# Erf's batches one step sooner than the mean's logarithms, and the forms of x one step behind their norm

## The chip, the cores and the metric

The kernel runs on one core of one Trainium2 chip. The metric is device time in microseconds of one execution. Small differences are told as a ratio with a 95% interval. Such a ratio is not quite the ratio of the medians quoted beside it.

## The reference, cut to what matters

```python
kv  = np.einsum('bhsd,bhse->bhde', k, v)          # 8 batches, 8 heads, 576 rows, 64 wide
out = np.einsum('bhsd,bhde->bhse', q, kv)
rms = np.sqrt(np.mean(out * out, axis=-1, keepdims=True) + 1e-06)
x   = (out / rms * g_norm)                        # -> 4608 x 512
h   = x @ w_in                                    # -> 4608 x 2048
sp  = np.maximum(h, 0.0) + np.log1p(np.exp(-np.abs(h)))   # softplus
y   = (h * erf(sp)) @ w_out                       # -> 4608 x 512
```

## The kernel before

The 4608 rows are worked on in nine groups of 512. The first two groups (T = 0 and 1) multiply in full precision; in their time the weights are unpacked (first group) and cut into three forms for the later groups (second group). A group has 16 steps, so there are 32 steps n; step n computes block n of h, and the projection of block n-5. Between them stand the pieces of the next group's attention: a pair of heads takes four steps, and its norm stands at the head of the step after them.

ScalarE's functions come from three tables here: softplus, erf, and one that has both exp and ln. Each change of table is an instruction. So erf is applied in batches of four blocks, and the mean's Ln and Exp stand between two loads.

```python
def mean():                                  # cut; step 4p+3
    nc.tensor.matmul(ms, lhsT=mean_w, rhs=st.pop("hi"), start=True, stop=False)
    nc.tensor.matmul(ms, lhsT=mean_w, rhs=st.pop("lo"), start=False, stop=True)
    exp_ln_table()
    nc.scalar.activation(r, ms, AF.Ln, bias=eps_col)
    nc.scalar.activation(r, r, AF.Exp, scale=-0.5)
    nc.scalar.activation(u, r, AF.Square)
    softplus_table()

def norm():                                  # step 4p+4: three VectorE operations
    ...                                      # L341 reads ms, L344, L353 reads o and writes x

def split():                                 # the three forms of x: one on ScalarE (L378),
    if T >= FIRST:                           # two on VectorE (L381, L382)
        thirds(st.pop("x"), *(x_forms[T][:, i, p, :] for i in range(3)))
```

```python
for n in range(FIRST * FC + 1):              # cut; FC = 16, BATCH = 4, LAG = 5
    for piece in steps[f][0]:
        piece()                              # attention of the next group, kv and qt first
    ...                                      # weights of the next steps
    nc.vector.tensor_tensor(out=hs[done], in0=hs[done], in1=ss[done], op=ALU.mult)  # done = n-4
    h_ps = ...                               # 4 matmuls (8 passes)
    nc.scalar.copy(h, h_ps)
    nc.scalar.activation(s, h, AF.Softplus)
    ...                                      # second group: forms of weights, two ahead of erf, one behind
    if f % BATCH == BATCH - 1:
        for i in range(n - BATCH + 1, n + 1):
            nc.scalar.activation(ss[i], ss[i], AF.Erf)
        softplus_table()
    ...
    project(f2, hs[n - LAG], last)
```

Two PSUM banks serve kv (the products of k and v), qt (q, transposed), se (kv applied to q) and ms (the mean's product) in turn: kv of a new pair takes the bank of the old ms, qt that of the old se.

## Time and profile before

| | |
|---|---|
| time | 991.83 us, median of 3 (991.8 to 993.1); in later rounds 989.9 to 990.1 |
| TensorE busy | 951.9 us of 991.4 (96%) |
| ScalarE, VectorE busy | 618.7 us (62%), 736.6 us (74%) |
| the 32 steps of the change | from 31.2 us, h of step 0, to 280.0 us, the first product of the part after it |
| TensorE's bracketed waits in steps 4 to 28 | 8.16 us: 1.49 + 0.59 + 3.45 in steps 4 and 5, 0.37 + 0.34 + 1.92 in step 24 and at the head of 25 |

A bracketed wait is the idle time that a profile line gives in brackets before an instruction, with what ended it. The page is read in this way: TensorE's busy share says that the end moves only with TensorE's gaps and its clock; the gaps in order of time say where; the engine named behind a gap says which stream to read next. The lines themselves are in the prediction.

### The profile page before, as it was taken

To read this page: it belongs to the slowest core of one execution; us is meant where nothing else is said; L and a number is where in the kernel's file an instruction comes from. 1 tells how busy PE (TensorE), PEld (TensorE's weight loads), DVE (VectorE), ACT (ScalarE), POOL (GpSimd) and SP (SyncE) were. 2 spreads that over 40 slices of the span, in tenths; PEclk is the share of its full clock that TensorE was granted. 3 is DMA by queue.
4 is the path that set the end of the run, shared out by engine and by line. 5 is a ranking of instruction groups with operands and counts; after the bars stand their busy time and mean duration, and the time that the engine had idled before them with its cause. 6 is when DMAs were issued, how large, how long until landed. Compare 5 with 4: busy or idle time off the path is not lost.

```text
span 991.4 us, 11745 instructions
## 1 busy us (share of the span) xinstructions
PE 951.9 (96%) x4328; PEld 681.5 (69%) x4328; DVE 736.6 (74%) x1047; ACT 618.7 (62%) x822; POOL 2.4 (0%) x10
## 2 busy tenths in 40 slices
PE   6779999989999999999999999999999999989997
PEld 4334444444477878787878787878787787768885
DVE  2887896657368887777777777888777787776666
ACT  3688776676466666666666666666666666665551
POOL 0000000000000000000000000000000000000000
PEclk9899999999999999999999999999999999999998
DMA  9755516679369976998689878977787678657952
GB/s 278 229 165 165 164 40 246 273 300 376 135 225 362 374 267 233 292 374 294 244 256 371 307 269 248 368 298 280 246 331 250 248 264 343 236 204 284 363 203 74
DMA packets 100936, 259.76 MB, mean 262 GB/s; under 512 B 44048, under 2 KB 57360, under 8 KB 100880
## 3 DMA queue, kind: packets, MB, share of 16 engines
q1 hardware_dynamic: 99248, 256.73, 72.4%
q10 hardware_dynamic: 1568, 2.29, 0.8%
q8 instruction: 34, 0.56, 0.2%
q14 instruction: 22, 0.18, 0.1%
q0 software_dynamic: 64, 0.00, 0.0%
HBM read 224.40 MB, written 34.60 MB: 261 GB/s over the span
## 4 chain that ended last, share of the span: by engine, by line
PE 72%; DVE 15%; ACT 7%; DMA 3%; issue 2%; SPq 0%; DVEq 0%; ACTq 0%
PE n_ps L427 34%; PE m_ps L427 17%; PE h_ps L582 7%; PE o_ps L464 6%; DVE h L718 3%; PE se_ps L304 3%; DVE e L412 2%; PE qt_ps L298 2%; PE kv_ps L276 1%; DMA w_out_parts<-w_out 1%; DVE u L344 1%; DVE x L353 1%; DVE u L341 1%; DVE e L407 1%; ACT L105 1%
## 5 line engine op out<-in xcount | busy, mean ns | idle before, releaser
L427 PE MATMUL n_ps<-x_forms,w_in_parts 128*128 128x512 f32 x896 | 234.2, 403 | 3.0 <-ACT x_forms L378 2.8
L427 PE MATMUL n_ps<-w_out_parts,g_forms 128*128 128x512 f32 x928 | 232.7, 393 | 3.0 <-DMA w_out_parts<-w_out 3.0
L427 PEld LDWEIGHTS n_ps<-w_out_parts,g_forms 128*128 128x128 f32 x928 | 175.6, 189 | 41.1 <-DMA w_out_parts<-w_out 3.8
L427 PEld LDWEIGHTS n_ps<-x_forms,w_in_parts 128*128 128x128 f32 x896 | 167.3, 189 | 47.6 <-issue 9.1
L702 ACT ACTIVATE s<-h 128x512 f32<-128x512 f32 x112 | 71.0, 634 | 200.1 <-DVE h L412 200.1
L427 PE MATMUL m_ps<-w_out_parts,g_forms 128*128 128x512 f32 x464 | 125.0, 391 | 0.0
L582 PE MATMUL h_ps<-xT,w_in_sb 128*128 128x512 f32 x256 | 121.2, 617 | 4.0 <-DVE qT L341 2.7
L427 PE MATMUL m_ps<-x_forms,w_in_parts 128*128 128x512 f32 x448 | 120.8, 392 | 0.0
L412 DVE TENSOR_TENSOR h<-m_ps,h 128x512 f32<-128x512 f32 x112 | 77.1, 688 | 50.4 <-ACT h L700 47.1
L381 DVE TENSOR_TENSOR g_forms<-h,g_forms 128x1024 fp32r<-128x1024 f32 x58 | 70.9, 1223 | 46.9 <-ACT g_forms L378 46.6
L464 PE MATMUL o_ps<-w_out_sb,h_sb 128*128 128x512 f32 x224 | 100.5, 592 | 0.0
L427 PEld LDWEIGHTS m_ps<-w_out_parts,g_forms 128*128 128x128 f32 x464 | 87.8, 189 | 18.4
L427 PEld LDWEIGHTS m_ps<-x_forms,w_in_parts 128*128 128x128 f32 x448 | 84.6, 189 | 17.7
L582 PEld LDWEIGHTS h_ps<-xT,w_in_sb 128*128 128x128 f32 x256 | 49.8, 198 | 63.4 <-issue 55.2
L412 DVE TENSOR_TENSOR e<-m_ps,e 128x512 f32<-128x512 f32 x116 | 80.3, 692 | 17.5 <-PE m_ps L427 9.3
L407 DVE SCALAR_TENSOR_TENSOR e<-n_ps,e 128x512 f32<-128x512 f32 x88 | 60.3, 686 | 28.8 <-PE n_ps L427 28.8
L464 PEld LDWEIGHTS o_ps<-w_out_sb,h_sb 128*128 128x128 f32 x224 | 42.5, 190 | 53.2 <-issue 49.5
L700 ACT ACTIVATE h<-n_ps 128x512 f32<-128x512 f32 x112 | 65.6, 586 | 17.3 <-PE n_ps L427 17.2
L382 DVE SCALAR_TENSOR_TENSOR g_forms<-g_forms 128x1024 fp32r<-128x1024 f32 x58 | 71.1, 1225 | 2.0
L378 ACT ACTIVATE g_forms<-h 128x1024 fp32r<-128x1024 f32 x58 | 61.2, 1054 | 10.0 <-DVE h L718 8.5
L718 DVE TENSOR_TENSOR h<-h,s 128x1024 f32<-128x1024 f32 x56 | 65.9, 1219 | 0.0
L105 ACT ACT_TABLE_LOAD x45 | 57.7, 1283 | 0.8
(82 smaller groups left out, 950.8 us busy)
## 6 DMA issues: line engine op xcount, KB each, us to landing
w_out_parts<-w_out SPq DMA_DIRECT2D x116, 768.0 KB, 7.5
w_in_parts<-w_in SPq DMA_DIRECT2D x112, 768.0 KB, 6.5
w_in<-w_new SPq DMA_DIRECT2D x16, 768.0 KB, 4.3
w_out<-w_new SPq DMA_DIRECT2D x16, 768.0 KB, 5.2
k_sb<-in_k_dram SPq DMA_DIRECT2D x29, 288.0 KB, 4.9
v_sb<-in_v_dram SPq DMA_DIRECT2D x29, 288.0 KB, 5.7
q_sb<-in_q_dram SPq DMA_DIRECT2D x32, 256.0 KB, 5.1
w_raw<-in_moe_w_out_dram SPq DMA_DIRECT2D x8, 1024.0 KB, 4.9
```

The costliest lines, as they stand in the source:

```text
L105: nc.scalar.preload_act_table_set("softplus")
L378: nc.scalar.activation(high, x, AF.Copy, scale=1.0 + 2.0**-13)
L381: nc.vector.tensor_tensor(out=low, in0=x, in1=high.bitcast(FP32), op=ALU.subtract)
L382: nc.vector.scalar_tensor_tensor(out=both, in0=low.bitcast(FP32), scalar=SHIFT, in1=high.bitcast(FP32), op0=ALU.mult, op1=ALU.add,)
L407: nc.vector.scalar_tensor_tensor(out=out_, in0=ps, scalar=scale, in1=out_, op0=ALU.mult, op1=ALU.add)
L412: nc.vector.tensor_tensor(out=out_, in0=ps, in1=out_, op=ALU.add)
L427: nc.tensor.matmul(ps, lhsT=weights(form, k), rhs=moving(form, k), start=(form == forms[0] and k == 0), stop=(form == forms[-1] and k == 3),)
L464: nc.tensor.matmul(o_ps[j], lhsT=g[:, j * P : j * P + P], rhs=w_out_sb[:, f, :], start=(f == 0), stop=last,)
L582: nc.tensor.matmul(h_ps, lhsT=w_in_sb[:, c, f * P : f * P + P], rhs=xT[T][:, c, :], start=(c == 0), stop=(c == KC - 1),)
L700: nc.scalar.activation(h[:, i], n_ps, AF.Copy, scale=SHIFT - 1.0)
L702: nc.scalar.activation(s[:, i], h[:, i], AF.Softplus)
L718: nc.vector.tensor_tensor(out=h[:, part], in0=h[:, part], in1=s[:, part], op=ALU.mult)
```

## The change

The intent: erf's batch stood in the same step as the mean, between the mean's table loads and the copy of qT that TensorE needs next. One step sooner, it should be out of the way of that copy. And the forms of x, which made VectorE wait for ScalarE in the step of the norm, are to come a step later.

```diff
-                steps[BATCH * p + BATCH][0][:0] = [norm, split]
+                steps[BATCH * p + BATCH][0][:0] = [norm]
+                if p < NP - 1:
+                    steps[BATCH * p + BATCH + 1][0].insert(0, split)
@@
+    erf_steps = (*range(2, FIRST * FC - BATCH, BATCH), FIRST * FC - BATCH, FIRST * FC - 1)
+    to_erf = []
@@
-            if f % BATCH == BATCH - 1:
-                for i in range(n - BATCH + 1, n + 1):
-                    nc.scalar.activation(ss[i], ss[i], AF.Erf)
+            to_erf.append(s)
+            if n in erf_steps:
+                for s in to_erf:
+                    nc.scalar.activation(s, s, AF.Erf)
+                to_erf.clear()
                 softplus_table()
```

The batches are then in steps 2, 6, ... 26, 28 and 31 in place of 3, 7, ... 31.

## The prediction

> **What bounds the kernel now.** I read the page's totals, then the slices, then TensorE's gaps in order of time through the part that the change touches, then ScalarE's and VectorE's order around each gap. In the totals (busy us, share of the span, instructions) TensorE is busy almost throughout:
>
> ```profile
> PE 951.9 (96%) x4328; PEld 681.5 (69%) x4328; DVE 736.6 (74%) x1047; ACT 618.7 (62%) x822; POOL 2.4 (0%) x10
> ```
>
> So only what opens or closes a gap of TensorE, or lowers its clock, moves the end. The change touches the first two groups: 32 steps, from about 31 to 278 us. A step is one block of h (8 MATMULs, 3.43 us), one block of the projection (another 3.43 us) and a piece of the next group's attention. A pair of heads takes four steps: its products (kv, qt) in step 4p, its application (se) in 4p+1, its halves in 4p+2, its mean in 4p+3, and its norm at the head of 4p+4. I number steps by counting ScalarE's copies of h (step 3 at 56.49 us, step 14 at 140.25, step 24 at 218.91). TensorE in order of time (start, duration, work, and in brackets the gap before it and what ended it) shows the only real gaps of group one after step 3:
>
> ```profile
> 53.95 0.92 PE L276 MATMUL kv_ps<-v_sb,k_sb 96*64 96x64 f32 x24 [1.49 <-DVE u L341]
> 55.47 0.66 PE L298 MATMUL qt_ps<-ident,q_sb 128*128 128x128 f32 x4 [0.59 <-DVE xT L353]
> ...
> 63.17 1.12 PE L304 MATMUL se_ps<-qT,bd_kv 128*128 128x512 f32 x2 [3.45 <-ACT qT L299]
> 64.13 5.29 PE L582 MATMUL h_ps<-xT,w_in_sb 128*128 128x512 f32 x8
> ```
>
> and of group two:
>
> ```profile
> 209.75 0.92 PE L276 MATMUL kv_ps<-v_sb,k_sb 96*64 96x64 f32 x24 [0.37 <-DVE u L341]
> ...
> 211.27 0.66 PE L298 MATMUL qt_ps<-ident,q_sb 128*128 128x128 f32 x4 [0.34 <-DVE x L353]
> ...
> 220.71 0.43 PE L303 MATMUL kv_ps<-qT_last,bd_kv 128*128 128x64 f32 x2 [1.92 <-DVE qT_last L294]
> ...
> 222.24 4.95 PE L582 MATMUL h_ps<-xT,w_in_sb 128*128 128x512 f32 x8
> ```
>
> Two things are to be seen. First, kv waits for the norm's first operation (L341) and qt for its last (L353), since they take the PSUM banks that these read; se waits for the copy of qT (L299), which in step 4 stands behind the erf batch. Second, after the gaps of 3.45 and 1.92 us eight MATMULs take 5.29 and 4.95 us in place of 3.60. So each of those gaps costs a further 1.7 to 1.8 us of clock. The 1.49 us gap cost none (the next eight: 3.60).
>
> ScalarE in order of time around the end of group one shows what is to be swapped:
>
> ```profile
> 140.85 0.63 ACT L594 ACTIVATE s_sb<-h_sb 128x512 f32<-128x512 f32 x1
> 141.50 1.28 ACT L102 ACT_TABLE_LOAD   x1
> 142.80 0.69 ACT L333 ACTIVATE rms_r<-ms_ps,eps_col 128x512 f32<-128x512 f32 x1
> ...
> 144.18 0.63 ACT L335 ACTIVATE u<-rms_r 128x512 f32<-128x512 f32 x1
> 144.83 1.28 ACT L105 ACT_TABLE_LOAD   x1
> 146.12 0.59 ACT L593 COPY h_sb<-h_ps 128x512 f32<-128x512 f32 x1
> ...
> 147.39 1.28 ACT L607 ACT_TABLE_LOAD   x1
> 148.68 2.19 ACT L607 ACTIVATE s_sb<-s_sb 128x512 f32<-128x512 f32 x4
> 150.89 1.28 ACT L105 ACT_TABLE_LOAD   x1
> 152.18 0.59 ACT L299 COPY qT<-qt_ps 128x512 f32<-128x512 f32 x1
> ```
>
> An erf batch with its two table loads is 1.28 + 2.19 + 1.28 = 4.75 us. It stands now after the mean and before the copy of qT.
>
> VectorE in order of time shows the cost of the early forms of x, which sit in its stream waiting for ScalarE, which is in its erf batch:
>
> ```profile
> 183.92 0.69 DVE L381 TENSOR_TENSOR x_forms<-x,x_forms 128x512 fp32r<-128x512 f32 x1 [7.36 <-ACT x_forms L378]
> ...
> 218.57 0.69 DVE L381 TENSOR_TENSOR x_forms<-x,x_forms 128x512 fp32r<-128x512 f32 x1 [7.36 <-ACT x_forms L378]
> ```
>
> The second of them is the cause of the 1.92 us gap: the copies of kv and of the q tail stand behind it.
>
> **What the Trainium skill says.** "ScalarE: Activation LUTs", section "What ACT_TABLE_LOAD costs", has about 1283 ns for a load and 1380 ns of drain besides. The trace has 45 loads of 1283 ns, but no drain: the softplus before 141.50 ends at 141.48, and the Ln starts at 142.80. I take 1.28. "TensorE: Matmul & The Clock Gate", section "Architectural detail: the array is 16× 32×32, not 1× 128×128", says that ScalarE and VectorE run their queues strictly in order. The trace agrees (the 7.36 us above), and so order is what this change is about. Its section "Part 1: The HAM clock gate (the "warmup" mystery)" says that TensorE falls to half clock after an idle window of about 3.4 us and that the window runs freely. The size fits here (1.7 us lost), while a gap of 1.92 us was enough, so I treat gaps between 1.5 and 3 us as a matter of chance.
>
> **The change part by part.** No arithmetic is removed. The erf batches (before: 8, in steps 3, 7, ... 31) become 9, in steps 2, 6, ... 26, 28 and 31: two more loads, 2.6 us of ScalarE late in group two, where it has idle stretches of 2.8 to 5.6 us, so nothing on the path. What moves: in each pair of steps 4.75 us pass from behind the mean (ahead of the qT copy) to ahead of it. The qT copy comes no later; Ln, Exp, Square, the norm, and with it kv and qt, come 4.75 us later, less what ScalarE idled there waiting for the mean's product. I replay each boundary with the durations of the rows.
>
> Step 4: three erfs, so 1.28 + 1.65 + 1.28 = 4.2 us. The Square ends at 57.4 in place of 53.2, kv starts at 58.2, qt at 59.7, h at 60.2. The gap becomes one of 5.7 us and the clock falls there. The softplus of step 3 ends at 62.0 and the qT copy at 62.5, while TensorE is in its slow h (60.2 to about 65.3). So the 3.45 us wait is gone, taken by the longer one: the projection starts at about 69.5 against 69.26. +0.2 us.
>
> Step 8: ScalarE had idled 1.36 us there, so the norm comes 3.4 us later; its first operation ends at 86.4 (kv is due at 87.0), its last at 87.9 (qt due at 88.0). Nothing. Step 12 likewise, 3.4 us later, qt at 118.54 against 118.40: +0.1.
>
> Step 16: no idling, so the Square ends at 144.81 + 4.75 = 149.56. VectorE, which was the later one at 147.0, now waits. Its first operation ends at 150.3, kv starts then in place of 148.01 (gap 2.3 us), the last ends at 151.8, qt starts at 151.86 in place of 149.25. +2.6 us, and I give a fall of the clock 6 chances in 10: +1.0.
>
> Step 20: Square at 179.2 in place of 174.3, since one form of a weight also lies behind the batch; kv at 179.95 in place of 178.86, qt at 181.46 in place of 179.71. +1.75 us.
>
> Step 24: here the split's move earns. VectorE no longer stands 7.36 us in step 20, so the weights' forms go out about 3.5 us sooner, and ScalarE's waits for them in steps 21 and 22 (3.80, 1.28, 1.27 us for transfers) mostly go, which pays for most of the erf batch. In TensorE's own time I get kv 0.95 us late and qt 0.35, a loss of 1.3 us. Before: 0.37 + 0.34 + 1.92 and about 1.8 of clock, 4.45. So −3.15 us.
>
> Step 28: Square ends at 244.5 in place of 240.0; kv at 245.25 in place of 244.75, qt at 246.75 in place of 245.60. +1.15 us.
>
> Sum: 0.2 + 0.1 + 2.6 + 1.0 + 1.75 − 3.15 + 1.15 = 3.65 us. After 280 us nothing moves but the start.
>
> **The rivals.** One: the shorter wait of the copy of qT is all gain, and the norm has room enough; then steps 4 and 24 give back 3.45 + 1.7 and 4.45, and the time is about 982 to 985. For it speaks that steps 8, 12, 20 and 28 have 3.5 to 4.0 us between the norm and kv. Against it: the batch is 4.75 us, and step 16 has 2.5 us. Two: the wait only changes its place, as I reckon for step 4, and in all the clock falls twice more than I count (steps 16 and 20): about 998 to 1000. That the gaps now are single waits between long stretches of work speaks for it. Three: steps 21 to 23 are bound by transfers (they move 400 to 440 GB/s around 190 to 205 us), so that the earlier forms do not come sooner; then step 24 keeps a gap of 3.4 us for kv and its fall of the clock, and the time is about 999. Against it: VectorE held them back for 7.36 us first.
>
> **Range and chances.** 991.83 + 3.65 = 995.5 us. Each fall of the clock is worth 1.7 us, three are in doubt (steps 16, 20, 24), and step 24 itself by 3 us either way: 990.0 to 1000.0 eight times in ten. A change of 2% would be 19.8 us, more than all gaps touched together (about 10 us before): within 2% 0.98, faster 0.01, slower 0.01.
>
> **What would show it.** 47 table loads in place of 45. TensorE's wait for the qT copy in step 5 gone, and one of about 5.7 us for L341 at kv in step 4. New waits for L341 and L353 at steps 16, 20 and 28 of about 2.3 + 0.3, 1.1 + 0.7 and 0.5 + 0.6 us. No wait for L294 in step 24, and no 4.95 us row after it. VectorE's two waits of 7.36 us for x_forms down to under 2. I would be wrong if kv starts in step 16 without a gap, or if step 24 still has one of over 2 us.

## The result, and the profile after

The changed kernel took 999.3 us (median of 4, 996.19 to 1000.61) against 991.82 us: ratio 1.0072, 95% interval 1.0044 to 1.0101, that is about 7.1 us more.

TensorE of the changed kernel in order of time, columns as in the prediction, first group (step 4, the se of step 5, step 16):

```profile
57.48 1.55 PE L276 MATMUL kv_ps<-v_sb,k_sb 96*64 96x64 f32 x24 [5.76 <-DVE u L341]
...
59.90 5.24 PE L587 MATMUL h_ps<-xT,w_in_sb 128*128 128x512 f32 x8
...
65.15 1.08 PE L304 MATMUL se_ps<-qT,bd_kv 128*128 128x512 f32 x2
...
150.83 0.92 PE L276 MATMUL kv_ps<-v_sb,k_sb 96*64 96x64 f32 x24 [2.32 <-DVE u L341]
...
152.35 1.12 PE L298 MATMUL qt_ps<-ident,q_sb 128*128 128x128 f32 x4 [0.34 <-DVE xT L353]
153.26 4.65 PE L587 MATMUL h_ps<-xT,w_in_sb 128*128 128x512 f32 x8
```

and second group (steps 20, 24 and 28):

```profile
184.60 0.92 PE L276 MATMUL kv_ps<-v_sb,k_sb 96*64 96x64 f32 x24 [1.11 <-DVE u L341]
...
187.02 4.84 PE L587 MATMUL h_ps<-xT,w_in_sb 128*128 128x512 f32 x8
...
218.55 0.92 PE L276 MATMUL kv_ps<-v_sb,k_sb 96*64 96x64 f32 x24 [1.11 <-DVE u L341]
...
220.86 4.98 PE L587 MATMUL h_ps<-xT,w_in_sb 128*128 128x512 f32 x8
...
251.88 0.92 PE L276 MATMUL kv_ps<-v_sb,k_sb 96*64 96x64 f32 x24 [0.46 <-DVE u L341]
```

The 3.45 us wait of se is gone and a 5.76 us wait of kv has come. Where before only one pair boundary of the second group waited, all now do, and for the norm (L341). Behind the waits of steps 4, 16, 20 and 24 the next block of h takes 4.65 to 5.24 us in place of 3.60. ScalarE of the changed kernel around step 15 shows why the norm is late: erf's batch and both of its loads are now ahead of the Ln.

```profile
143.25 2.19 ACT L613 ACTIVATE s_sb<-s_sb 128x512 f32<-128x512 f32 x4
145.46 1.28 ACT L105 ACT_TABLE_LOAD   x1
146.75 1.28 ACT L102 ACT_TABLE_LOAD   x1
148.04 0.69 ACT L333 ACTIVATE rms_r<-ms_ps,eps_col 128x512 f32<-128x512 f32 x1
...
149.43 0.63 ACT L335 ACTIVATE u<-rms_r 128x512 f32<-128x512 f32 x1
```

The two traces can be set side by side from the first block of h (31.19 us before, 30.44 after), by the start of the work that follows each boundary (the last column is what the waits leave over, about the excess of the slow rows):

| boundary | predicted | measured | of it waits | of it clock (about) |
|---|---|---|---|---|
| step 4 and 5 | +0.2 | +0.98 | +0.2 | +0.8 |
| step 8 and 12 | +0.1 | +0.20 | +0.2 | 0 |
| step 16 | +3.6 | +4.13 | +2.66 | +1.5 |
| step 20 | +1.75 | +3.49 | +1.7 | +1.8 |
| step 24 | −3.15 | −1.46 | −1.18 | −0.3 |
| step 28 | +1.15 | +1.20 | +1.05 | 0 |
| sum | +3.65 | +8.54 | | |

The bracketed waits of these steps are 12.62 us after and 8.16 before: 4.46 more. My own terms without those for the clock come to 0.2 + 0.1 + 2.6 + 1.75 + (1.3 − 2.63) + 1.15 = 4.47. So the replay of the waits was right in these two profiles, and what was missed is clock. The span rose by 5.8 us, not 8.54: the changed kernel's first step began 0.75 us sooner, and the part after the 32 steps took 709.4 us against 711.4, a difference that a later run puts down to chance (the second profile of the kernel before, below).

### The profile page after: what moved, and what is told of

The parts are those of the page before. It is cut to its first block, busy times and chain, and to the rows that moved or that the text cites. A ratio compares the mean times of both kernels' runs of the same rounds, so it can differ in the third digit from the quotient of the medians.

```text
span 997.2 us, 11743 instructions
## 1 busy us (share of the span) xinstructions
PE 954.0 (96%) x4328; PEld 683.0 (68%) x4328; DVE 736.9 (74%) x1047; ACT 621.0 (62%) x824; POOL 2.4 (0%) x10
## 4 chain that ended last, share of the span: by engine, by line
PE 70%; DVE 15%; ACT 9%; DMA 4%; issue 1%; SPq 1%; DVEq 0%; ACTq 0%
PE n_ps L427 34%; PE m_ps L427 17%; PE h_ps L587 6%; PE o_ps L464 4%; DVE h L725 3%; PE se_ps L304 3%; DVE e L412 2%; PE qt_ps L298 2%; PE kv_ps L276 2%; DVE u L341 1%; DVE u L344 1%; ACT s_sb L613 1%; DVE x L353 1%; DMA w_out<-w_new 1%; ACT L102 1%
## 5 line engine op out<-in xcount | busy, mean ns | idle before, releaser
L587 PE MATMUL h_ps<-xT,w_in_sb 128*128 128x512 f32 x256 | 123.4, 627 | 4.0 <-DVE qT L341 2.7
L105 ACT ACT_TABLE_LOAD x46 | 59.0, 1283 | 0.8
```

What stands on the lines that cost most here:

```text
L105: nc.scalar.preload_act_table_set("softplus")
L587: nc.tensor.matmul(h_ps, lhsT=w_in_sb[:, c, f * P : f * P + P], rhs=xT[T][:, c, :], start=(c == 0), stop=(c == KC - 1),)
```

## The experiments

Theories: A, the time follows TensorE's gaps at the boundaries and the falls of its clock behind them; B, moving erf also does what the split's move was for, so that the second has nothing left to earn; C, the slow rows are the clock falling because TensorE idled. Their rivals are given with each run.

**1. The split's move alone.** Only the first hunk of the diff. 

```diff
-                steps[BATCH * p + BATCH][0][:0] = [norm, split]
+                steps[BATCH * p + BATCH][0][:0] = [norm]
+                if p < NP - 1:
+                    steps[BATCH * p + BATCH + 1][0].insert(0, split)
```

> The forms of x one step later, erf left where it was. Theory A (the gaps of TensorE and the falls of its clock make the whole difference, and VectorE's stand of 7.36 us for the forms causes the 1.92 us gap of step 24): kv's and qt's small waits of step 24 (0.37, 0.34) and the 1.92 us wait go, and with them the slow row after it: 4.4 us less than the kernel before, about 987.4, the first batch's gaps in steps 4 and 5 unchanged. Rival (step 24 is bound by the transfers of the weights' forms, which saturate the DMA engines, so that freeing VectorE does nothing): within 1 us of the kernel before, and a wait of over 1 us left in step 24.

Measured: 986.08 us against 990.04, ratio 0.9957 (0.994 to 0.9975). The second group has no bracketed wait left; kv's second part at the head of step 25, which waited 1.92 us before, starts straight behind the projection:

```profile
216.54 0.33 PE L303 MATMUL kv_ps<-qT_last,bd_kv 128*128 128x64 f32 x2
```

This part of the change is thus good by itself by 4.3 us, and its rival (the transfers) falls.

**2. Erf's move alone.** The other hunks, with `[norm, split]` left together.

> erf's batches one step sooner, the forms of x left where they were. Rival (as I predicted: the split's move earns 3 us in step 24): about 3 us slower than the changed kernel, some 1002, with a wait of over 1.5 us for L294 or a kv wait of over 3 us in step 24. Theory B (once erf no longer stands between the norm and the forms, VectorE's stand for them falls to about 2 us by itself, so that the split's move has nothing left to earn): within 1 us of the changed kernel, about 999, no wait for L294, and VectorE's waits for x_forms about 2 us.

Measured: 997.64 us against 990.04, ratio 1.0073 (1.0053 to 1.0093), the changed kernel's own ratio. The waits are the same as the changed kernel's to 0.02 us, with the same four slow blocks of h. VectorE in this kernel at step 24:

```profile
223.39 0.69 DVE L381 TENSOR_TENSOR x_forms<-x,x_forms 128x512 fp32r<-128x512 f32 x1 [2.44 <-ACT x_forms L378]
```

With erf gone from between the norm and the forms, VectorE waits 2.44 us in place of 7.36 without any move of the split. Theory B holds: the waits are alike, and the two ratios agree within intervals of some 2 to 3 us each way, so the 4.3 us of the first experiment are not there to be had once erf has moved. Erf's move alone takes 0.0116 (1.0073 − 0.9957) more than the split's move alone.

**3. and 4. Erf's move in one group alone.** Both with the forms later. Each has one of the two new lines; the comments are added here.

```diff
-    erf_steps = (*range(2, FIRST * FC - BATCH, BATCH), FIRST * FC - BATCH, FIRST * FC - 1)
+    erf_steps = (3, 7, 11, 15, 18, 22, 26, FIRST * FC - BATCH, FIRST * FC - 1)   # second group only
+    erf_steps = (2, 6, 10, 14, 15, 19, 23, 27, FIRST * FC - 1)                   # first group only
```

> The changed kernel with the first group's erf batches back in steps 3, 7, 11 and 15, and only the second group's sooner (18, 22, 26, 28, 31). Theory A: the losses of step 4 (1.0 us net) and step 16 (2.6 of waits and 1.5 of clock) go, those of steps 20, 24 and 28 stay, step 20's smaller by the 0.55 us of one erf: about 5 us less than the changed kernel, some 994. Rival (the 47 loads, or the second part of the kernel, cost the time, not the boundaries): the same as the changed kernel within 1.5 us.

> The complement of the second-group-only kernel: erf's batches sooner in the first group alone (2, 6, 10, 14), the one block left over in step 15, then 19, 23, 27 and 31 as before; the forms of x later. Theory A (boundaries add up): step 4 +1.0, step 12 +0.2 and step 16 +4.1 (2.6 of waits, 1.5 of clock) from the changed kernel's trace, step 24 -4.4 from the forms-later kernel: +0.9 us on the kernel before, ratio about 1.001. Rival (the group's shift against the transfers eats the second group's gain): ratio 1.004 or more, with a wait of over 1 us at step 24.

Measured: second group alone 989.45 us against 990.04, ratio 1.0002 (0.9976 to 1.0027); first group alone 993.13 against 989.92, ratio 1.0032 (1.0018 to 1.0046). Against the forms-later kernel (0.9957) the first group costs 0.0075, the second 0.0045, together 0.0120, and both at once 0.0115: the boundaries add up. The first-group kernel has no wait at step 24, so its rival's mechanism is absent, though its ratio of 1.0032 lies nearer the rival's 1.004 than my 1.001. Both of my figures were off by some 2 us, in opposite directions. For the first-group kernel this is probably because I reckoned from the first profile of the kernel before, which fell in a run some 3 us slower than its usual one. For the second-group kernel the clock fell nowhere in steps 4 to 28 of its profile; that was one of two runs with a granted clock of 0.997, and the other four had 0.990 to 0.993, so this explains its median only in part. This is TensorE of that kernel at step 24:

```profile
210.24 0.92 PE L276 MATMUL kv_ps<-v_sb,k_sb 96*64 96x64 f32 x24 [1.45 <-DVE u L341]
...
212.24 3.60 PE L587 MATMUL h_ps<-xT,w_in_sb 128*128 128x512 f32 x8
```

A gap of 1.45 us at kv with no slow block behind it, where the changed kernel's of 1.11 us had one. In the same profile the 3.44 us wait of se in step 5 also left the clock alone, while in the kernel before and in the forms-later one the same wait did not.

**5. The waits filled.** The changed kernel with MATMULs that nobody needs in the waits ahead of kv. They write into the bank of the coming block of h, whose first real MATMUL overwrites them. (The diff is cut: the old line that allocates `h_ps` goes.)

```diff
+            h_ps = ps_h.tile([P, G], FP32, name="h_ps", tag="h")
+            for _ in range({4: 6, 16: 2, 20: 1, 24: 1}.get(n, 0)):
+                nc.tensor.matmul(h_ps, lhsT=ident, rhs=xT[T][:, 0, :], start=True, stop=True)
             for piece in steps[f][0]:
                 piece()
```

> The changed kernel with idle MATMULs (results overwritten) on TensorE in the waits before kv: six in step 4, two in step 16, one each in 20 and 24, each pair of passes about 0.86 us, all shorter than the wait they fill, so kv starts no sooner. Theory C (the slow rows after these waits are the clock falling because TensorE idled): the slow rows of steps 4, 16, 20 and 24 are gone (8 MATMULs in 3.6 us again) and the time is 7 us less than the changed kernel, about 992, though no other engine does anything sooner. Rival (the slow rows come from what the other engines or transfers do then, or from the free-running window whatever is filled): the rows stay at 4.7 to 5.2 us and the time is the changed kernel's within 1.5 us.

Measured: 992.33 us against 990.04, ratio 1.0021 (1.0007 to 1.0035), 5.1 us better than the changed kernel for more work on its busiest engine. TensorE at step 4:

```profile
51.62 5.31 PE L579 MATMUL h_ps<-xT,ident 128*128 128x512 f32 x12
57.54 0.92 PE L276 MATMUL kv_ps<-v_sb,k_sb 96*64 96x64 f32 x24 [0.61 <-DVE u L341]
...
59.55 3.60 PE L589 MATMUL h_ps<-xT,w_in_sb 128*128 128x512 f32 x8
```

From the first block of h, kv starts at 27.03 us here and 27.04 in the changed kernel, so nothing else is sooner, and yet the block of h behind it is at full speed. The same at steps 16, 20 and 24. Theory C holds. Its 7 us were too many: in the traces the 32 steps are 5.8 us shorter, because at step 24 TensorE, now earlier, waits for the norm again (1.27 us besides the filling). The six runs spread by 0.7 us (992.15 to 992.88), the changed kernel's four by 4.4. In the second experiment, in the same rounds and with the changed kernel's waits, they spread by 5.1: from 1000.53 us at a granted clock of 0.983 to 995.39 at 0.989. So a good part of the scatter between runs is probably falls of the clock.

**6. The changed kernel a second time.**

> The changed kernel once more, for a second profile. Theory C2 (whether a gap of 1 to 3.5 us lowers the clock depends on where it falls in a free-running window, which moves little against the kernel's own steps from one run to the next): gaps the same to 0.1 us, the slow rows of steps 4, 16, 20 and 24 mostly there again but not surely, each worth about 1.7 us. Rival (length of the gap decides): the same four, no more and no fewer.

Measured: 999.99 us, one run. The waits were the first profile's to 0.02 us and the same four blocks of h slow (5.45, 4.77, 4.91 and 5.06 us). The falls thus come again, but both profiles are of runs near the median; the fastest run of the changed kernel (996.19 us, granted clock 0.988 in place of 0.983 to 0.986) probably had fewer. And length alone does not decide: over all kernels that move erf in the second group kv's gap of step 24 is 1.10 to 1.12 us where the clock fell behind it (three profiles: this one, the first, and erf's move alone) and 1.24 to 1.45 where it did not (three kernels, of which those of experiments 5 and 8 have other work just ahead of the gap). This run alone cannot tell the rival apart; experiments 3 and 5 do.

**7. The kernel before a second time.**

> The kernel before once more, for a second profile. Theory: the first two groups as in the first profile to 0.2 us apart from one fall of the clock more or less (steps 5 and 24), and the part after them, which the change doesn't touch, 2 us shorter than the 711.4 us of the first profile, as in all the other profiles (707 to 710). Rival: 711 us again, so that the change did shorten the part after it by 2 us.

Measured: 994.5 us, one run. The waits of steps 4, 5 and 24 are 1.48, 0.59, 3.44, 0.36, 0.34 and 1.92, as before, and the part after the 32 steps took 708.5 us. So the 2 us that the changed kernel seemed to gain there are no work of the change. The early steps, though, were 3 us longer in this profile (another fall of the clock and a longer gap in steps 0 and 1), which I had not expected. Both profiles of the kernel before also fell in slow runs for it: 993.2 and 994.5 us at granted clocks of 0.987 and 0.988, where most of its runs take about 990 at 0.990 to 0.991. So its usual run probably has one or two falls fewer than these profiles show (an estimate: 0.003 of 990 us is 3 us, and a fall is worth about 1.7), and the clock's part in the table above is that of one pair of runs.

**8. The block of h ahead of kv.** The changed kernel with TensorE's own order turned round in steps 4, 8, 12, 20, 24 and 28.

```diff
+            h_early = f % BATCH == 0 and f > 0
+            if h_early:
+                h_ps = h_block(T, f)         # the 4 matmuls of the block
             for piece in steps[f][0]:
                 piece()
@@
+            if not h_early:
+                h_ps = h_block(T, f)
```

> The changed kernel with TensorE's own order changed in steps 4, 8, 12, 20, 24 and 28: the block of h (3.43 us) ahead of kv and qt. Theory D (a later norm costs only because kv and qt, which need its banks, stand first in TensorE's order): the waits for L341 and L353 at steps 20, 24 and 28 are gone, that of step 4 falls from 5.8 to about 2.3 us, step 16 keeps its 2.3: about 10 us less than the changed kernel, a ratio to the kernel before of about 0.997. Rival (the copy of qT, now behind the block of h in time, makes se wait instead): the waits reappear at se, and the ratio stays over 1.003.

Measured: 993.5 us against 990.1, ratio 1.0051 (1.0024 to 1.0077). A miss: by the ratios about 2 us of the 10 foretold. The wait of step 4 fell to 2.33 us and that of step 20 went, as expected, but se then waited 1.95 us for the copy of qT in step 5, as the rival said, and steps 24 and 28 kept theirs (1.24 and 0.70 us). TensorE in step 24, and before it ScalarE in step 20:

```profile
220.28 0.92 PE L276 MATMUL kv_ps<-v_sb,k_sb 96*64 96x64 f32 x24 [1.24 <-DVE u L341]
```

```profile
197.40 0.63 ACT L396 ACTIVATE w_new<-w_in_sb 128x512 fp32r<-128x512 f32 x1 [5.24 <-DMA w_in<-w_new]
```

The trace suggests how the 3.43 us were lost again: VectorE waits for the later kv (1.77 us) ahead of the weights' forms, these go out later, and ScalarE waits 5.24 us for a transfer to give back its buffer where it waited 0.90 before, so erf and the norm behind it are later too. No run isolates that.

**9. Forms later, and the first batch of erf moved the other way.** The forms-later kernel, with the batch of step 3 not sooner but behind step 4's copy of qT.

```diff
-            if f % BATCH == BATCH - 1:
+            if f % BATCH == BATCH - 1 and n != BATCH - 1:
@@
             for piece in steps[f][0]:
                 piece()
+            if n == BATCH:
+                for i in range(BATCH):
+                    nc.scalar.activation(ss[i], ss[i], AF.Erf)
+                softplus_table()
```

> The kernel before with the forms of x one step later, and of the erf batches only the first moved, and the other way: behind step 4's copy of qT, not ahead of the mean. Theory A: the wait of se for that copy (3.44 us) goes, and with it most falls of the clock behind it (1.7 us where they come); VectorE's and ScalarE's weights bound steps 5 and 6 then, so 3.5 to 5 us less than the forms-later kernel alone, ratio to the kernel before about 0.991, some 982. Rival (the first batch is bound by ScalarE's whole work there, so the wait only changes its place again, as it did in the changed kernel): the same as the forms-later kernel alone within 1 us, ratio 0.995 to 0.996.

Measured: 981.7 us against 990.1, ratio 0.9914 (0.9899 to 0.9929). This beats both kernels: 8.4 us under the kernel before. TensorE in steps 5 and 6:

```profile
58.99 1.08 PE L304 MATMUL se_ps<-qT,bd_kv 128*128 128x512 f32 x2
...
67.40 3.67 PE L588 MATMUL h_ps<-xT,w_in_sb 128*128 128x512 f32 x8 [0.47 <-DVE w_in_sb L227]
```

Se no longer waits, the clock did not fall, and what remains in steps 5 and 6 is 0.47 us for VectorE's weights. Step 4 keeps its 1.49 and 0.59 us.

**10. The same with the block of h ahead of kv.**

> Both: the forms later, the first erf batch behind step 4's copy of qT, and the block of h ahead of kv. Theory: the 1.49 and 0.59 us of step 4 go too, but VectorE's weights bound step 6 at nearly the same time, so at most 1 us less than the same without h first. Rival (each gap closed is worth its length): 2 us less.

Measured: 985.31 us against 990.1, ratio 0.9948 (0.9934 to 0.9963). Slower than without it by 3.4 us; neither figure was right. The waits of step 4 went (1.49 and 0.59), step 6 then waited 1.50 us for the weights, and in step 25 se waited 1.45 us for the copy of qT. ScalarE's order ahead of that copy is the same in both kernels, but its waits for transfers in steps 20 and 21 were 5.04 and 4.17 us in place of 1.61 and 2.63; as in experiment 8, no run isolates that.

## Why the prediction was right, and where it was not

The time was in the range and the direction was right: 999.3 us against 995.5 predicted, in a range of 990 to 1000. The size was not: about 7.1 us more where 3.65 had been reckoned. The median lies 0.7 us inside the range, one of the four runs (1000.61) outside it, and what kept it inside is the width that the range had for the clock's falls; so far that is luck. By its own steps:

- **Erf's batch goes from behind the mean to ahead of it, and kv and qt come later by what ScalarE does not idle away.** Right at every boundary: kv's waits of 5.76, 2.32, 1.11, 1.11 and 0.46 us against 5.7, 2.3, 1.1, 0.95 and 0.5 foretold, and none at steps 8 and 12.
- **Step 4 changes one wait for another.** Right; the 5.76 us replaced 1.49 + 0.59 + 3.45. Rival one, in which the wait of the copy is all gain, falls for this change. Its size was not idle, though: moving the batch the other way (experiment 9) brings 981.7 us, just under the 982 to 985 that it had said.
- **The falls of the clock: the term that was mis-sized.** I put down "a matter of chance" for gaps between 1.5 and 3 us and gave only step 16 a part of one (+1.0), none to step 20, and counted step 24's as gone. In both profiles of the changed kernel the clock fell at steps 4, 16, 20 and 24, at the last two behind gaps of 1.11 us. It cost 1.5 at step 16, 1.8 at step 20, left only 0.3 of the 1.8 to be saved at step 24, and cost 0.8 more than before at step 4, since the longer wait came with a longer fall (half clock for about 6.8 us by the clock's record, in place of 3.4). Together that is some 4.6 of the 4.9 us by which the 8.54 exceed my sum. Rival two had this ("the clock falls twice more than I count (steps 16 and 20): about 998 to 1000") and I took it for a rival only, though I gave step 16's fall 6 chances in 10.
- **"Here the split's move earns."** The wait for L294 went and VectorE was freed, as I wrote, but the reason was wrong in one point: with erf moved, the split's move adds nothing (1.0073 without it, 1.0072 with it). I had not asked what the split's move is worth once erf has moved.
- **VectorE's waits for the forms down to under 2 us.** Wrong, and of no weight: the trace of the changed kernel has 2.07 and 5.89 us in steps 21 and 25, now behind the copies that TensorE needs.
- **Rival three, the transfers.** It falls: ScalarE's waits for transfers there were 0.90 and 1.91 us (steps 20 and 21), where the kernel before had 3.80, 1.28 and 1.27, and in step 24 kv waited 1.11, not 3.4.
- **"47 table loads in place of 45."** A misreading: that is one row of the page, the loads of softplus at one line, which went to 46. With the other lines there were 114 loads before and 116 after. The difference of two was right.
- **The base.** 991.83 us was a little high; in later rounds the kernel before took about 990.0.

What stays open: why the clock fell behind 1.11 us at step 24 and not behind 1.45. The free-running window that the Trainium skill describes ("TensorE: Matmul & The Clock Gate", section "Part 1: The HAM clock gate (the "warmup" mystery)") would fit it, but no run set the phase of that window, so this is not shown.

## What to carry to other kernels

Moving a block of work on an in-order engine takes it off one consumer's path and puts it on another's; before the move, look up the slack of whatever it is put in front of (here 2.5 to 4.0 us, for a batch of 4.75). Of two changes that cure the same wait, test each alone: here one was worth 4.3 us, the other cost about 11 on top of it, and together they looked like one mild loss. And price a gap of TensorE at its length plus a possible fall of the clock, about 1.7 us: here one came behind gaps of 1.11 us, and none behind others of 1.24 to 1.49. Where the wait can't be removed, MATMULs without use in it can bring part of the loss back.

## What the Trainium skill lacked or had wrong

- "ScalarE: Activation LUTs", section "What ACT_TABLE_LOAD costs": the load of 1283 ns is right, the further 1380 ns of drain are not to be seen. In the lines of ScalarE above two loads and the start of the Ln are 1.29 us apart each (145.46, 146.75, 148.04).
- "TensorE: Matmul & The Clock Gate", section "HAM oscillation — how this bites in real kernels": its rule is no idle gaps over about 3.4 us. Here the clock fell behind a gap of 1.11 us followed by kv's small MATMULs and one of 0.34 us, and once did not fall behind one of 3.44 us. (The page's next section tells of short idles that do the same, without a length.) The size agrees: this is the kernel before behind the 3.45 us wait, each stretch with its length, the busy times of PE, PEld, DVE, ACT and POOL, then TensorE's clock, the DMA share and GB/s. By the clock column it ran at half clock for about 3.4 us, so 1.7 us were lost.

```profile
64.00:65.00 1.00, 1.00 (x3) 0.53 (x2) 0.80 (x1) 1.00 (x2) 0.00 (x0) 0.77 0.00 0
65.00:66.00 1.00, 1.00 (x2) 0.34 (x1) 1.00 (x2) 0.97 (x3) 0.00 (x0) 0.50 0.00 0
66.00:67.00 1.00, 1.00 (x2) 0.34 (x1) 0.97 (x2) 1.00 (x3) 0.00 (x0) 0.50 0.00 0
67.00:68.00 1.00, 1.00 (x3) 0.36 (x2) 1.00 (x2) 1.00 (x2) 0.00 (x0) 0.53 0.26 51
68.00:69.00 1.00, 1.00 (x4) 0.52 (x3) 0.97 (x3) 0.72 (x1) 0.00 (x0) 1.00 0.81 211
```

- No page that I read for this case says that idle MATMULs in a wait pay: ten of them (20 passes) took the changed kernel from a ratio of 1.0072 to 1.0021 and its scatter from 4.4 to 0.7 us.
